# A two-layer network behind a linear-attention scan: all eight first-layer banks by float32r parts, VectorE makes the parts of x, attention buffers shared, new order from step 3 on

## The chip, the cores and the metric

The kernel runs on one core of one Trainium2 chip. The metric is device time in microseconds (us) of one execution. The kernel before takes 586.06 us, the median of 3 runs (585.86 to 586.9).

## The reference

An attention block with a decaying state is followed by a network of two layers. Shapes: 4 batches, 8 heads, 768 positions, 48 dimensions a head; 3072 tokens of 384 features; 2048 hidden units. All is float32.

```python
f = 1.0 / (1.0 + np.exp(-f_logit))
for t in range(S):
    state = f[:, :, t, :, None] * state + np.einsum('bhd,bhe->bhde', k[:, :, t], v[:, :, t])
    y[:, :, t] = np.einsum('bhd,bhde->bhe', q[:, :, t], state)
...
x = y.transpose(0, 2, 1, 3).reshape(B * S, H * D)
h = x @ w_in
g = np.maximum(h, 0.0) + alpha * np.minimum(h, 0.0)
return g @ w_out
```

## The kernel before

**Steps.** The work is cut into 12 steps, numbered 0 to 11. A step is a pair of batches and a chunk of 128 positions: 256 tokens. Each step has an attention part and a network part. The attention of step n+1 runs among the network of step n.

**Order.** Every engine runs its instructions in the order of one list, `ORDER_WORDS`, written out in the program. A word such as `5R0` is the part `R0` of step 5; `5Nb3` is the part `b3` of step 5's network; words without a number (`Y3`, `Z3`, `S3`, `W2`, `T`) prepare the weights. A part that yields is spread over several words of the same name. Each word issues on one engine or queue, so the list fixes the order on TensorE, VectorE, ScalarE, GpSimd and SyncE alone, and waits between engines follow from who reads and writes which bytes. Transfers are issued from SyncE's queue (outputs, turned keys, x) and from GpSimd's queue (loads of f, q, k, v for the steps after the first).

**Attention.** Words that the change and the prediction touch:

- `ef`, `eq`, `ek`, `ev`: loads of f, q, k, v (L369, L386). `f` (L396 to L403): sigmoid of f on ScalarE and three copies. `F` (L410 to L421): products of neighbouring decays on VectorE. `g` (L439 to L444): ScalarE copies to the first part of `scores`. `G` (L458, L462): scans over blocks of four, which read a constant pattern `ones`.
- `h`, `i`, `k` (L469, L490, L500, L496, L504, L578): scaled keys and queries and, from step 2 on, VectorE's transpose of the keys; it goes into the buffer in which f was. `K` (L584): the turned keys go through DRAM.
- `p`, `q` (L544): from step 2 on, six products that write queries shifted by one to seven quarters into `scores`. `u0`, `u1` (L705): 64 instructions on TensorE that multiply keys with these. `r0`, `r1` (L696): the same for positions within a quarter.
- `R0`, `R1` (L715) and `U0`, `U1` (L560): VectorE's predicated copies of both results from PSUM into the small buffer `ad`. `A0`, `A1` (L724): ScalarE copies `ad` into the score matrix `A`.
- `d` (L648), `D`, `M` (L659, L666): increments of the state and its update. `y` (L733), `Y` (L602): the outputs y. `X` (L611 to L614): y goes through DRAM to the layout `xT`, 384 features by 256 tokens (the last step by ten smaller transfers, L747).

**Network.** The hidden layer is cut into eight banks of 256 units. A bank is six products of 128 by 128 weights with 256 columns of x (L955) in one PSUM bank. In steps 0 to 2 all banks are plain float32 (`Na`). From step 3 on (`PARTS = 3`) banks 2 to 7 (`SPLIT = 2, 8`) are computed from float32r parts in three passes: `hi` with the high part of x, `lo` with the low part (both `Na`), a scaling of the bank in place on ScalarE (`Nq`, L969), and `sum` with a mix of x (`Nb`). Banks 0 and 1 stay plain. The parts of the weights are made once (`Y`, `Z`, `S`: L896, L900, L902, L906).

The parts of x are made in each step: `Nx` (ScalarE, L941) rounds x to `xh`; `Ny` and `Nz` (ScalarE, L944) copy it scaled to `xl` and `xs`; `NY` and `NZ` (L947) are accumulating transfers from GpSimd's queue that add x to `xl`, and `xl` to `xs`.

Behind each bank ScalarE writes the negative side (`Nr`, L979) and VectorE the gate in two halves (`Nc`, L986). The second layer is done with seven block products of 16 instructions each (`Np`, L1013) of sums of gate blocks (`Nm`, `Nu`, `Nv`, `Nw`, L1007). VectorE and ScalarE gather the results in `o` (L1023, L1044, L1048); `NL` is the last of these. `Ns0` and `Ns1` store `o` (L891) from SyncE's queue.

Of the kernel before, what the change touches and what calls it, by code (L numbers as in the profile page):

```python
# [8 lines left out]
F32 = mybir.dt.float32  # L9
F32R = mybir.dt.float32r  # L10
# [8 lines left out]
C = 128  # L19
# [3 lines left out]
U = 2  # L23
# [12 lines left out]
SPLIT = 2, 8  # L36
TURNED = SPLIT[1] - SPLIT[0]
# [4 lines left out]
0ef 0eq 0ek 0ev 0ev a0 a1 0f a2 0f 0F b0 0f a3 0F 0F 0F 0F 0I0 0F 0g 0g 0G 0G 0r1 0g 0G 0G 0g 0r0 1ef 0g 0I1 0g 0h 0I2  # L42
a0 0I3 0I4 a0 0i 0I5 a1 0m a4 1eq a1 0p 0p 1ek 0p 0p a2 1ev b1 0p 0j 1ev a2 0l 0o a5 0l 0O 0R0 0O 0k 0O 0R0 0O 0R0 0R0
0q 0q 0u0 0s 0s 0s 0t 0s w0 0t 0J0 0K0 0U0 0U0 0J1 0U0 0R1 0H0 0H0 0R1 0J2 0H0 0R1 0H0 1f 0R1 w1 0u1 1f 1f 0K1 0J3 0U1
2ef 0A0 0U1 0A0 0U1 1F 0d 0A0 1F 0A0 1F 0J4 0D 1F 0D 0J5 1F 0H1 0H1 1F 0H1 0H1 w2 0A1 0y0 0A1 1G 1G 0A1 0J6 0A1 1G 1G
0Y0 b0 0y1 b0 0x0 0M 2ev 0Y1 a6 2ev 1g 0M 1g 0J7 0M 1g 1r0 1g 1i 1g 0x1 1g 1R0 1R0 0X 0X 1R0 1r1 0X 1R0 a3 1h 0Na0 a3
a4 2eq a7 w3 a4 2ek 1m 0Na1 b1 b2 w4 b1 1R1 1R1 a5 a6 0Na3 1p 1p 1p b3 a6 1R1 1p 1j 1R1 1s 0Nr1 0Nr3 a5 1s 0Nc1 0Nc3
0Nc3 0Na2 w5 1p 1t 2f 0Nc1 b4 0Na4 w6 0Nr2 0Nc2 1l a7 0Nr4 0Nc2 0Na5 1t 1s 1l 1k 1s a7 b2 w7 0Nr0 1K1 1o 0Nc4 0Nr5
0Nc5 b2 b4 0Nc0 0Na6 1O 1O 1O 0Na7 b3 0Nc0 v0 1q 0Nc5 b4 v1 b7 0Np0 0Nr6 1K0 0Nc4 b5 b5 1q 1u0 b3 v2 1O v3 1U0 1u1 1U0
1U0 b5 1U1 2f 2f 2F 1H0 1H0 2F 1H0 1H0 2g 2F 2F 2F 0Np1 2g 2f b7 1U1 0Nc6 b6 b7 2F 2G v4 v5 1d v7 0Nr7 b6 2g 0Np2 2G  # L50
2g 1D 1D b6 1U1 1A0 2h 2p 1H1 2p 1H1 V 1H1 0Nc7 0Nc7 1H1 0Nc6 v6 W1 W0 2q 1A0 1A0 W3 1A0 0Np3 0Np4 0Np5 2q 1y0 W2 1A1
1A1 1A1 1A1 2h Y2 2g 2q 1y1 1Y1 1Y0 0Np6 1M 0Np7 2q 2u0 1M 2G 2G 1M W4 2i 1X 1X 1X 1X 1X 1X 1X 1X 1X 2r0 2R0 1X 2i
1Na1 2R0 2i 2R0 2R0 2U0 2U0 2U0 2k Y4 2k 1Nr1 0No1 0No0 2U0 2U0 1Na2 2U0 1Nr2 Y3 2U0 2A0 1Na0 3ef 2l 2l W6 2r1 1Nr0 2l
W5 2A0 1Nc1 2K 1Nc0 2A0 1Nc0 2o 2t 2K 2l 1Na5 2D 2K 2l 1Nr5 1Nc5 1Na4 1Nc1 Z4 Z4 1Na3 2t 1Nc5 2O 2A0 2R1 Z2 2R1 1Na6
# [105 lines left out]
def kernel(  # L160
# [985 lines left out]
```

## Time and profile before

| what | value |
|---|---|
| median of 3 runs | 586.06 us |
| the profiled execution's own time | 585.39 us |
| its span, from first to last instruction | 583.6 us |
| mean granted TensorE clock | 0.985 |
| GpSimd, accumulating transfer to `xl` (L947) | 9 of 934 ns on the queue |
| ScalarE, idle before rounding x (L941), ended by the transfer of x | 23.9 us in 8 waits |

PE is TensorE's matmuls, PEld its weight loads, DVE VectorE, ACT ScalarE, POOL GpSimd, SP SyncE. The digits of a slice are tenths of busy time in a fortieth of the span. In a group's row stand line, engine, operation, output and inputs by their names, shapes and count, then busy us and the mean ns of one, then the idle time before them and what ended it. Matmuls overlap, so one that lasts 380 ns does not hold TensorE for 380 ns: what counts is the time from one start to the next.

### The profile page before, as it was taken

What the parts mean: (1) busy time and instruction counts of PE and PEld (TensorE: products, weight loads), DVE (VectorE), ACT (ScalarE), POOL (GpSimd) and SP (SyncE); (2) the same over time, 40 slices, a digit from 0 to 9 for tenths busy, and PEclk for the clock granted to TensorE, in tenths of its full rate; (3) what the DMA queues carried; (4) which work ended last, traced back from release to release, by engine and by line L of the source; (5) the groups of instructions that cost most, each with busy time, mean ns of one, the idle gap of its engine ahead of it and who ended that gap; (6) DMA issues with size and microseconds to landing.
All of it is one profiled execution on the core that took longest, in us unless ns stands there. A gap on an engine that the chain in (4) does not pass through costs nothing.

```text
span 583.6 us, 19142 instructions
## 1 busy us (share of the span) xinstructions
PE 570.9 (98%) x8308; PEld 525.9 (90%) x8308; DVE 499.5 (86%) x1055; ACT 317.6 (54%) x593; POOL 63.4 (11%) x104
## 2 busy tenths in 40 slices
PE   8799999999999999999999999999999999999997
PEld 6678767899899899999899999999999999999997
DVE  6888799999999899999999899989998979864262
ACT  5698883673372582483384284385384284372230
POOL 5202000200100111111010100111111100101000
PEclk9679999999999999999999999999999999999999
DMA  9938501630713553543633542743542641512200
GB/s 287 357 120 297 218 1 57 164 90 12 190 35 82 93 173 96 113 154 104 134 110 80 105 150 66 151 145 88 105 155 62 136 150 55 93 52 65 60 1 27
DMA packets 69444, 67.59 MB, mean 116 GB/s; under 512 B 44688, under 2 KB 58640, under 8 KB 69360
## 3 DMA queue, kind: packets, MB, share of 16 engines
q1 hardware_dynamic: 59744, 37.16, 22.9%
q0 software_dynamic: 8880, 28.84, 18.7%
q8 instruction: 65, 1.06, 0.7%
q10 hardware_dynamic: 736, 0.37, 0.2%
q14 instruction: 19, 0.16, 0.1%
HBM read 44.99 MB, written 13.50 MB: 100 GB/s over the span
## 4 chain that ended last, share of the span: by engine, by line
PE 65%; DVE 14%; ACT 2%; DMA 2%; issue 2%; SPq 0%; DVEq 0%; POOLq 0%
PE ph L955 28%; PE pa L1013 8%; PE pc L1013 4%; PE pb L1013 4%; PE pf L1013 4%; PE pe L1013 4%; PE pd L1013 4%; PE py L733 3%; PE qu L705 3%; DVE scores L544 2%; DVE gate L1007 2%; PE raw L696 2%; PE inc L648 2%; DMA f<-in_fT 1%; DMA turned<-f 1%
## 5 line engine op out<-in xcount | busy, mean ns | idle before, releaser
L979 ACT ACTIVATE gate<-ph 128x512 f32<-128x512 f32 x96 | 56.0, 596 | 107.0 <-PE ph L955 77.4
L986 DVE SCALAR_TENSOR_TENSOR gate<-gate,om,ph 128x256 f32<-128x256 f32 x192 | 84.9, 474 | 26.8 <-ACT gate L979 26.2
L1007 DVE TENSOR_TENSOR gate<-gate 128x512 f32<-128x512 f32 x88 | 59.1, 685 | 13.2 <-PE pb L1013 6.3
L955 PE MATMUL ph<-xT,w_in_sb 128*128 128x256 f32 x288 | 66.0, 380 | 0.0
L1013 PE MATMUL pa<-w_out_sb,gate 128*128 128x192 f32 x352 | 61.3, 327 | 0.0
L955 PEld LDWEIGHTS ph<-xT,w_in_sb 128*128 128x128 f32 x288 | 53.7, 190 | 6.9 <-issue 0.2
L1013 PEld LDWEIGHTS pa<-w_out_sb,gate 128*128 128x128 f32 x352 | 57.4, 190 | 0.3
L969 ACT ACTIVATE ph<-ph 128x512 f32<-128x512 f32 x54 | 30.7, 579 | 38.0 <-PE ph L955 32.0
L955 PE MATMUL ph<-xh,hi 128*128 128x256 f32 x324 | 49.0, 288 | 1.9 <-DVE o L1023 1.0
L955 PE MATMUL ph<-xT,w_in_split 128*128 128x256 f32 x216 | 48.6, 381 | 0.0
L560 DVE COPY_PREDICATED ad<-inq,qu 128x224 f32<-128x224 int32 (+6 forms) x140 | 41.9, 300 | 7.0 <-PE qu L705 3.6
L955 PE MATMUL ph<-xl,lo 128*128 128x256 f32 x324 | 47.7, 285 | 0.0
L955 PEld LDWEIGHTS ph<-xh,hi 128*128 128x128 f32 x324 | 42.4, 190 | 4.2 <-issue 1.5
L955 PEld LDWEIGHTS ph<-xT,w_in_split 128*128 128x128 f32 x216 | 40.6, 190 | 5.6
L955 PE MATMUL ph<-xs,sum 128*128 128x256 f32 x324 | 44.0, 281 | 0.0
L955 PEld LDWEIGHTS ph<-xl,lo 128*128 128x128 f32 x324 | 42.6, 191 | 0.3
L724 ACT COPY A<-ad 32x256 f32<-32x256 f32 x88 | 35.3, 401 | 10.7 <-DVE ad L560 9.5
L715 DVE COPY_PREDICATED ad<-mraw,raw 128x256 f32<-128x256 int32 (+1 forms) x88 | 38.9, 442 | 2.6 <-ACT A L724 0.7
L955 PEld LDWEIGHTS ph<-xs,sum 128*128 128x128 f32 x324 | 40.1, 188 | 0.6 <-ACT ph L969 0.2
L544 DVE TENSOR_TENSOR scores<-scores,q 128x768 f32<-128x768 f32 (+5 forms) x60 | 37.3, 621 | 0.8
L1013 PE MATMUL pb<-t,gate 128*128 128x192 f32 x176 | 31.0, 330 | 0.0
L1013 PE MATMUL pc<-t,gate 128*128 128x192 f32 x176 | 30.8, 328 | 0.0
(150 smaller groups left out, 1067.4 us busy)
## 6 DMA issues: line engine op xcount, KB each, us to landing
w_out_raw<-in_w_out SPq DMA_DIRECT2D x8, 767.8 KB, 11.8
w_in_raw<-in_w_in SPq DMA_DIRECT2D x8, 767.2 KB, 10.6
f<-in_fT POOLq DMA_DIRECT2D x11, 512.0 KB, 6.9
q<-in_qT POOLq DMA_DIRECT2D x11, 512.0 KB, 5.9
k<-in_kT POOLq DMA_DIRECT2D x11, 512.0 KB, 6.3
turned<-f SPq DMA_DIRECT2D x40, 128.0 KB, 3.4
ksn<-turned SPq DMA_DIRECT2D x10, 512.0 KB, 4.0
out<-o SPq DMA_DIRECT2D x24, 192.0 KB, 3.7
```

What stands on the lines that cost most here:

```text
L544: nc.vector.tensor_tensor(by_four(us[:, :, UO[m]:UO[m] + 4 * n]), by_four(us[:, :, skip:skip + 4 * n]), spread(fq[:, :, 1:1 + n], n), ALU. ...
L560: nc.vector.copy_predicated(to, inq[:, 0:NB - m].bitcast(I32).unsqueeze(1).unsqueeze(3) .broadcast_to((128, H, NB - m, 4)), of)
L705: nc.tensor.matmul(qu[DB * j:DB * (j + 1), par, hp * QS + 4:hp * QS + QL], lhsT=x["k4"][r_, g * DB:(g + 1) * DB], rhs=x["us"][r_, g, 4:QL] ...
L715: nc.vector.copy_predicated(adu[:, :, :, d:4], diag[:, :, 0:n].bitcast(I32).unsqueeze(1).broadcast_to((128, H, NB, n)), rv[:, :, QO[d]:QO[ ...
L724: nc.scalar.copy(A[s_, u, :, s_], ad[s_].rearrange("p r h t -> p (r h) t"))
L733: nc.tensor.matmul(py[64 * par:64 * par + 64, u, o:o + CH], lhsT=vs_flat[bp][:, at_:at_ + 64], rhs=A[:, u, par * HP + hp, CH * cc:CH * (cc ...
L955: nc.tensor.matmul(banks[f][:, j * T:(j + 1) * T], lhsT=of[:, kt, 128 * j:128 * (j + 1)], rhs=by[:, kt], start=first_ and kt + j == 0, sto ...
L969: nc.scalar.activation(banks[f], banks[f], AF.Copy, scale=EPS - 1.0)
L979: nc.scalar.activation(to, of, AF.Relu, scale=-1.0)
L986: nc.vector.scalar_tensor_tensor(to[:, j], to[:, j], om[:, m:m + 1], of[:, j], ALU.mult, ALU.add)
L1007: nc.vector.tensor_tensor(block(to)[:, p], block(x_)[:, p], block(y_)[:, p], op)
L1013: nc.tensor.matmul(banks[to][:, 0:DH], lhsT=block(of)[:, f], rhs=of_w_out(by)[:, f], start=start and f == 0, stop=f == NH - 1, skip_group_ ...
```

## The change

All eight banks are computed by parts from step 3 on, so banks 0 and 1 get `hi`, `lo` and `sum` as well, two scalings a step more, and six more products of weight preparation. `xl` goes: VectorE makes the low part in the place of x (`NY`) and the mix (`NZ`); the two copies `Ny`, `Nz` and the accumulating transfers go.

To make room, buffers are shared. `scores` becomes four segments of 1024 columns: seven shifted queries lie in 28 of each 32 columns; `ad` lies in the four columns left over in segments 1 and 2; f is loaded into segment 3. The transposed keys go into q's buffer, `kh` into `q3`'s first part, and the scans' `ones` into spare columns of q's buffer, written by ScalarE in each step. The output `o` of a step uses the buffer of the mix `xs`. Part `i` gives one of its operations to `k`. The signs of the high parts are turned, so that the remaining operations are additions. The order list is new from the middle of step 1's attention on; ahead of that only the loads `1ef` and `2ef` stand later.

```diff
-SPLIT = 2, 8
-TURNED = SPLIT[1] - SPLIT[0]
+PIECES = 8
...
+    SEG = DB - 4
+    PLACES = {1: (0, 4), 2: (1, 4), 7: (1, 28), 3: (2, 4), 6: (2, 24), 4: (3, 4), 5: (3, 20)}
...
+    scores = const.tile([128, 4 * W], F32, tag="scores", name="scores")
+    segs = scores.rearrange("p (s g t) -> p s g t", s=4, t=DB)
...
+    ad = scores.rearrange("p (h i t) -> p h i t", i=NB, t=DB)[:, 4:12, :, 0:4]
...
-            t = work.tile([128, W], F32, tag=name, name=f"{name}_{i}", bufs=1)
+            t = scores[:, 3 * W:4 * W] if name == "f" else work.tile([128, W], F32, tag=name, name=f"{name}_{i}", bufs=1)
...
-            nc.scalar.copy(x["fs"][:, 0:NS:NB + 1], ones[:, 1:2].broadcast_to((128, G + 1)))
+            nc.scalar.copy(x["fs"][:, 0:NS:NB + 1], one[:, 1:2].broadcast_to((128, G + 1)))
+            yield
+            nc.scalar.copy(x["ones"].rearrange("p (g i) -> p g i", i=NB + 1), one.unsqueeze(1).broadcast_to((128, G // 2, NB + 1)))
...
+                        nc.tensor.matmul(qu[DB * j:DB * (j + 1), par, hp * C:hp * C + 4 * SEG].rearrange("p (s t) -> p s t", s=4),
+                                         lhsT=x["k4"][r_, g * DB:(g + 1) * DB], rhs=segs[r_, :, g, 4:DB], start=True, stop=True)
...
         def fourth():
+            ended(1, x)
+            yield
+            started(1, x)
+
+        def fifth():
             ended(0, x)
             yield
-            ended(1, x)
-            yield
-            started(1, x)
-
-        def fifth():
             carried(x)
             yield
-            nc.vector.transpose(x["kt"], x["ks"].rearrange("p g s t -> p (g s t)"))
+            nc.vector.transpose(x["q"], x["ks"].rearrange("p g s t -> p (g s t)"))
...
         def high_of_x():
-            nc.scalar.activation(late["xh"], x["T"], AF.Copy, scale=ROUND)
-
-        def part_of_x(to, scale):
-            nc.scalar.activation(late[to], late["xh"].bitcast(F32), AF.Copy, scale=scale)
-
-        def rest_of_x(to, of):
-            nc.gpsimd.dma_start(out=late[to].bitcast(F32), in_=of.bitcast(F32), accum_op=ALU.add)
...
+            nc.scalar.activation(late["xh"], x["T"].bitcast(F32), AF.Copy, scale=-ROUND)
+
+        def low_of_x():
+            nc.vector.tensor_tensor(x["T"], x["T"].bitcast(F32), late["xh"].bitcast(F32), ALU.add)
+
+        def mix_of_x():
+            x["xs"] = late["parts"].tile([128, NK, T], F32R, tag="xs", name=f"xs_{i}")
+            nc.vector.scalar_tensor_tensor(x["xs"], late["xh"].bitcast(F32), -EPS, x["T"].bitcast(F32), ALU.mult, ALU.add)
...
-            if by_parts(f):
-                products(f, late["hi"][:, f - SPLIT[0]], late["xh"], True, False)
+            if n_ >= PARTS:
+                products(f, late["hi"][:, f], late["xh"], True, False)
                 yield
-                products(f, late["lo"][:, f - SPLIT[0]], late["xl"], False, False)
+                products(f, late["lo"][:, f], x["T"], False, False)
...
+        def side_(r):
+            if "o" not in x:
+                x["o"] = late["parts"].tile([128, U, DM], F32, tag="xs", name=f"o_{i}")
+            return x["o"][:, r]
...
-            parts.update(x=high_of_x, y=lambda: part_of_x("xl", -1.0), z=lambda: part_of_x("xs", EPS),
-                         Y=lambda: rest_of_x("xl", x["T"]), Z=lambda: rest_of_x("xs", late["xl"]))
+            parts.update(x=high_of_x, Y=low_of_x, Z=mix_of_x)
```

The list itself is over a thousand words long. Three places of it are spoken of below. The stretch from step 9's last output word to step 10's mix, new:

```
9NL 9Ns0 11l 11r1 11l 11t 11t 11t 11l 11t 10Na1 11U0 11l 11U0 10NY 10Na3 10Na4 10Na4 10NZ
```

The words of step 10's network behind the last `11U1`, old, then new (words of step 11 left out):

```
Nc0 Nr4 Nc0 Nr3 Nb2 Na5 Nc4 Nr2 Na6 Nc3 Na6 Nq6 Nc4 Na7 Nq5 Na7 Nc2 Nc3 Nb6 Nb5 Nq7 Nr5 Nc2 Nb7 Nc5 Nc5 Nr7 Nr6 Nc6 Nc6 Nc7 Nc7 Np0 Nm0 Np2 Nu0 Nv0 Nk Np3 Ng Nm1 Nu1 Nv1 Np1 Nw0 Nw1 Np6 Np4 Np5 Nd Ne Nf Nh Nj Nl Ni NL Ns0 Ns1
Nr5 Nc6 Nc6 Nb7 Nr7 Nc7 Np0 Nc7 Nm1 Nc5 Nc5 Np2 Nu0 Nv0 Nk Nu1 Np3 Np1 Nw0 Nw1 Np6 Nv1 Np4 Nd Ne Ng Nh Nj Np5 Nf Ni Ns1 Nl NL Ns0
```

The load of f of step 10 stands as `9u0 ... 9u1 ... 10ef 10f`, with the other words of step 9 and of step 8's network between them.

More of the change, by code (lines that the diff above doesn't have):

```diff
@@ L50 @@
[L50 to L54, printed above, removed]
@@ L971, in third_pass @@
         def third_pass(f):
-            products(f, late["sum"][:, f - SPLIT[0]], late["xs"], False, True)
+            products(f, late["sum"][:, f], x["xs"], False, True)
         def sides(f):
```

289 lines of the change are left out of this document (144 added, 145 removed).

## The prediction

> **What bounds the kernel now.** I read the page first, then windows of busy time, then the order of time on TensorE.
>
> ```profile
> span 583.6 us, 19142 instructions
> ...
> PE 570.9 (98%) x8308; PEld 525.9 (90%) x8308; DVE 499.5 (86%) x1055; ACT 317.6 (54%) x593; POOL 63.4 (11%) x104
> ...
> PE   8799999999999999999999999999999999999997
> ...
> DVE  6888799999999899999999899989998979864262
> ...
> PE 65%; DVE 14%; ACT 2%; DMA 2%; issue 2%; SPq 0%; DVEq 0%; POOLq 0%
> ```
>
> TensorE is busy almost everywhere and carries 65% of the chain of waits. But VectorE's slices are also nines from 80 us to 510 us; its free time lies at both ends. The same in three stretches (columns: length, then busy us and instruction count of PE, PEld, DVE, ACT, POOL, then clock, DMA share, GB/s):
>
> ```profile
> 80.00:160.00 80.00, 79.74 (x1085) 67.98 (x1084) 77.99 (x158) 41.17 (x79) 7.22 (x11) 1.00 0.35 92
> 80.00:513.40 433.40, 430.12 (x6631) 401.08 (x6630) 403.78 (x866) 231.22 (x440) 46.33 (x63) 1.00 0.42 106
> 513.40:583.60 70.20, 66.75 (x563) 65.45 (x561) 30.58 (x67) 22.14 (x43) 2.86 (x4) 1.00 0.15 40
> ```
>
> I cut at 513.40 because VectorE's last attention copy of step 11 (word 11U1) ends there:
>
> ```profile
> 511.89 1.46 DVE L560 COPY_PREDICATED ad<-inq,qu 128x160 f32<-128x160 int32 x5
> ```
>
> Behind it stands a tail whose length TensorE sets (66.75 of 70.20). Ahead of it VectorE is busy 403.78 of 433.40, 93%, and from 80 to 160 us even 77.99 of 80, 97.5%, with TensorE at 79.74. So this is a kernel bound by TensorE with a second engine close behind, and the change takes from the first and gives to the second.
>
> **TensorE's gain per bank.** A first-layer bank is six products. In plain float32 each is two instructions, by parts three (parts of x times hi, lo, sum). Starts in order of time, from the tail, where nothing waits:
>
> ```profile
> 543.89 2.75 PE L955 MATMUL ph<-xT,w_in_sb 128*128 128x256 f32 x12
> 546.29 1.07 PE L955 MATMUL ph<-xh,hi 128*128 128x256 f32 x6
> 547.19 0.88 PE L955 MATMUL ph<-xl,lo 128*128 128x256 f32 x6
> 547.91 0.88 PE L955 MATMUL ph<-xh,hi 128*128 128x256 f32 x6
> 548.63 0.88 PE L955 MATMUL ph<-xl,lo 128*128 128x256 f32 x6
> 549.35 0.84 PE L955 MATMUL ph<-xs,sum 128*128 128x256 f32 x6
> 550.03 0.88 PE L955 MATMUL ph<-xh,hi 128*128 128x256 f32 x6
> ```
>
> A hi or lo pass takes 0.72 us from start to start (547.91, 548.63, 549.35), a sum pass 0.68 (549.35 to 550.03): 2.12 us per bank. The plain bank and the hi pass behind it take 3.30 (543.89 to 547.19), so the plain bank takes 3.30 - 0.72 = 2.58. Gain: 0.46 us per bank. Banks 0 and 1 change in steps 3 to 11, 18 banks: 8.3 us. The lower bound comes from the groups' own busy time, which charges the change of kind between groups to the parts:
>
> ```profile
> L955 PE MATMUL ph<-xT,w_in_sb 128*128 128x256 f32 x288 | 66.0, 380 | 0.0
> L955 PE MATMUL ph<-xh,hi 128*128 128x256 f32 x324 | 49.0, 288 | 1.9 <-DVE o L1023 1.0 <-DVE gate L986 0.6
> L955 PE MATMUL ph<-xl,lo 128*128 128x256 f32 x324 | 47.7, 285 | 0.0
> L955 PE MATMUL ph<-xs,sum 128*128 128x256 f32 x324 | 44.0, 281 | 0.0
> L955 PEld LDWEIGHTS ph<-xT,w_in_sb 128*128 128x128 f32 x288 | 53.7, 190 | 6.9 <-issue 0.2
> L955 PEld LDWEIGHTS ph<-xh,hi 128*128 128x128 f32 x324 | 42.4, 190 | 4.2 <-issue 1.5 <-ACT gate L979 1.4 <-ACT ph L969 0.4
> ```
>
> 66.0 / 24 banks = 2.75 against (49.0 + 47.7 + 44.0) / 54 = 2.61: 0.14 x 18 = 2.6 us. I take 8.3, since starts are what the next matmul sees. The quarter products keep 112 columns in four pieces of 28: no new price.
>
> The weight loads speak against the gain: 12 x 53.7 / 288 = 2.24 us of load time for a plain bank, 18 x 42.4 / 324 = 2.36 by parts. The Trainium skill, Perfetto Trace Analysis, Identifying the Most-Contended Engine, says that matmul busy time misjudges TensorE's headroom and that the busy share of weight loads is the better measure. By that rule the 18 banks would cost 18 x 0.12 = 2.2 us more instead of 8.3 less; the passes above, at 0.72 us for six loads whose own records are 190 ns each, speak against it.
>
> **VectorE's new work.** Today x's parts are made by two copies on ScalarE and two accumulating DMAs from GpSimd's queue. Now VectorE makes both: one two-input operation over 768 columns each.
>
> ```profile
> L902 DVE SCALAR_TENSOR_TENSOR lo<-w_in_split,lo 128x768 fp32r<-128x768 f32 x6 | 5.7, 950 | 0.0
> L906 DVE TENSOR_TENSOR sum<-lo,hi 128x768 fp32r<-128x768 f32 x6 | 5.8, 966 | 0.4 <-PE ph L955 0.4
> L986 DVE SCALAR_TENSOR_TENSOR gate<-gate,om,ph 128x256 f32<-128x256 f32 x192 | 84.9, 474 | 26.8 <-ACT gate L979 26.2
> L1007 DVE TENSOR_TENSOR gate<-gate 128x512 f32<-128x512 f32 x88 | 59.1, 685 | 13.2 <-PE pb L1013 6.3 <-PE pc L1013 6.0
> L659 DVE TENSOR_TENSOR vs<-vs,f 48x768 f32<-48x768 f32 x20 | 19.1, 953 | 1.8 <-PE py L733 1.3
> ```
>
> The two forms cost 0.95 us, as L902 and L906 show for the same size. Ahead of 11U1 lie steps 3 to 10: 16 x 0.95 = 15.2 us. The two further pieces of w_in need a lo and a sum each: 2 x (0.95 + 0.97) = 3.8. The transposed keys, the carried keys and the predicated copies keep their counts and sizes; only addresses change.
>
> **What the new order moves across the cut.** Behind the last 11U1 the old order has nine first-layer passes of step 10 (second pass of bank 5, both of 6 and 7, third of 2, 5, 6, 7); the new one has only the third of bank 7. That is 5 x 0.72 + 3 x 0.68 = 5.6 us of TensorE moved ahead of the cut. Seven gating operations go with them (7 x 84.9 / 192 = 3.1 us of VectorE), one half of a gate sum (0.67) and one state product (0.95). Step 11's increments (64 small matmuls) go behind it:
>
> ```profile
> L648 PE MATMUL inc<-vs,ksn 64*48 64x48 f32 x768 | 11.9, 213 | 0.2 <-ACT A L687 0.2
> ```
>
> That is 11.9 / 12 = 1.0 us back into the tail.
>
> **Work that costs nothing, and its cover.**
>
> ```profile
> L944 ACT ACTIVATE xl<-xh 128x768 fp32r<-128x768 f32 x9 | 7.5, 838 | 0.2
> L969 ACT ACTIVATE ph<-ph 128x512 f32<-128x512 f32 x54 | 30.7, 579 | 38.0 <-PE ph L955 32.0 <-DVE gate L986 2.8 <-ACT A L526 1.6
> L398 ACT COPY k<-f 128x256 f32<-128x256 f32 x12 | 8.0, 663 | 2.0 <-PE qu L705 1.7
> ```
>
> Per step ScalarE loses two copies like L944's (1.68 us) and gains two bank scalings (1.16) and one copy of ones, at most L398's 0.66. That is even; ScalarE is busy 231 of 433 us, and without that cover 0.2 us a step would show. The 18 accumulating DMAs leave GpSimd's queue, so its loads of f, q, k, v no longer stand behind them. That is a relief for a queue that sets nothing now. The new waits are these:
>
> ```profile
> f<-in_fT POOLq DMA_DIRECT2D x11, 512.0 KB, 6.9
> out<-o SPq DMA_DIRECT2D x24, 192.0 KB, 3.7
> xT<-tokens SPq DMA_DIRECT2D x9, 384.0 KB, 3.2
> ```
>
> f now lies in the fourth quarter of the scores buffer, so its load can start only when the previous step's quarter matmuls (u1) are through; in the order u1 stands some 6 us of VectorE work ahead of the load, and ScalarE's sigmoid 0 to 3 us behind it, except 13 us in step 4. With 6.9 us to landing, the sigmoid may wait 4 to 7 us. Queued behind it on ScalarE are gate and A copies; ScalarE has 200 us free in the stretch, so I take zero and keep 1 us a step, 8 us, as the other end. xT is now overwritten in place, so its next load waits for the last lo pass; at least 11 us of VectorE work between y's copy and the first part, in steps 3 to 10, cover the two transfers. The outputs share the mix's buffer: see the third rival.
>
> **The sum.** Ahead of the cut VectorE has 403.8 + 15.2 + 3.8 + 3.1 + 0.67 + 0.95 = 427.5 us. At the 97.5% of 80 to 160 us this takes 438.5, which is 5.1 more than 433.4; with no gap at all 427.5, 5.9 less. TensorE there has 430.1 - 16 x 0.46 + 5.6 - 1.0 = 427.3, which at 79.74 of 80 takes 428.7: 4.7 less, so this is the floor. I take 436, +2.5: nearer to the row that shows VectorE full, a little under it since the row holds waits as well. The tail loses 5.6 and step 11's 2 x 0.46 = 0.9, and gets 1.0 back: -5.5. Together -3.0 on the profiled execution's 585.39 us (span 583.6 and 1.8 around it): 582.4. The runs' median, 586.06, is 0.67 above that execution, so 583.0 us.
>
> **Rivals.** *First, VectorE's work finds its gaps.* With VectorE taking 428.7 or less, TensorE sets the stretch: -4.7 - 5.5 gives 575.2, with the offset 575.9. For it: TensorE missed only 0.26 us from 80 to 160 us although VectorE was full. Against: it needs VectorE above 99% for 430 us.
>
> *Second, the weight loads set the pace.* TensorE gains nothing and pays 2.2 us: 586.06 + 2.2 = 588.3, slower by 0.4%. The rule of the skill quoted above would have it so; the 0.72 us passes speak against it.
>
> *Third, slower: the mix waits for the store.* The mix of step n+1 is written where step n's output lies, so VectorE must wait until the last store has landed, 3.7 us after its issue. In the new order, between the word that finishes the output (NL) and the mix (NZ), little lies on VectorE. In step 10 it is this, with the first part's 0.95:
>
> ```profile
> L509 DVE TENSOR_TENSOR q<-q,q 128x512 f32<-128x512 f32 x10 | 6.9, 686 | 0.1
> L496 DVE TENSOR_TENSOR q<-scores,q 128x512 f32<-128x512 f32 x20 | 13.5, 675 | 0.0
> L560 DVE COPY_PREDICATED ad<-inq,qu 128x224 f32<-128x224 int32 x20 | 8.2, 409 | 4.0 <-PE qu L705 3.6
> ```
>
> With two copies near L560's 0.4 and two operations under 0.2 us that is 3.4 us; in steps 7 to 9 the same count gives about 3.6, in steps 4 to 6 between 4.3 and 5.0. Once VectorE is full, whatever is missing stops the attention copies and gate operations queued behind the mix, and so PSUM banks and TensorE. At 0.5 us for wake-up and issue besides the landing it is under 1 us a step; with SyncE's queue late, since each store stands behind a transfer that waits for another, 1 us in each of 8 steps: 583.0 + 8 = 591. It decides as soon as VectorE has no gap left to repay, and today's waits show that it is not free of them:
>
> ```profile
> DVE gate L986 <- ACT gate L979: 9.3, 14, 1.9
> DVE ad L560 <- PE qu L705: 3.6, 3, 1.9
> ```
>
> These are waits from 80 to 513.4 us (total, times, longest): 12.9 us in which VectorE already waits for ScalarE and TensorE.
>
> **How the numbers follow.** My forecast, VectorE as the second bound at 583.0 (its own range 580 to 587), has 0.45; the first rival 0.18, the second 0.07, the third 0.30. The time is the likeliest's. A change under 0.2%, 1.2 us, is not told from none here. Of the forecast's 0.45 some 0.30 is faster by more than that, 0.10 within and 0.05 slower; the first rival is all faster; the second is 0.02 within and 0.05 slower; the third 0.03 within and 0.27 slower. Faster 0.48, same 0.15, slower 0.37. The range reaches from just under the first rival to above the third: 575.5 to 593.5.
>
> **What would show it.** In the changed profile, 2.1 us from start to start for every bank of steps 3 to 11; VectorE near 520 us busy in all and at 97% from 160 us to the last 11U1; that word at about 516 us, then 65 us of tail. If VectorE waits for out's store ahead of the mix in most steps, the third rival holds. I am wrong altogether if ScalarE's sigmoid waits for f by more than it has free, or if VectorE stays under 95% while TensorE too falls below 97%.

## The result, and the profile after

The changed kernel takes 588.86 us, the median of 20 runs (587.04 to 591.13); the kernel before took 586.69 us beside it, 20 runs (585.26 to 589.14). The ratio is 1.0035, interval 1.0021 to 1.0049: slower by 0.35%. The forecast was 583.0 us, faster by 0.5%. The profiled execution took 590.55 us, with a span of 588.8 us. It lies 1.7 us above the median of its kernel, and the profiled execution of before (585.39 us) 1.3 us below the one beside it: some 3 of the 5.2 us by which the spans differ are spread between executions, and the stretches below hold them.

First the page of the changed kernel: busy time of each engine, slices of TensorE and VectorE, and the shares of the chain of waits.

```profile
span 588.8 us, 19396 instructions
...
PE 565.6 (96%) x8416; PEld 520.8 (88%) x8416; DVE 515.3 (88%) x1077; ACT 320.7 (54%) x607; POOL 50.2 (9%) x89
...
PE   8789989999999999989999999999999999999996
...
DVE  6888798989999999989999989999999999984452
...
PE 24%; DVE 11%; issue 1%; DMA 1%; ACT 0%; DVEq 0%; ACTq 0%; SPq 0%
```

TensorE lost 5.3 us of busy time (570.9 before), VectorE gained 15.8 (499.5), and the span grew by 5.2. TensorE's share of the chain fell from 65% to 24% (the shares of the new chain sum to 37%, so it was followed back only part of the way; TensorE to VectorE is 65 to 14 before and 24 to 11 after). Between 404 and 424 us the chain of the changed kernel, in order of time, is almost VectorE alone:

```profile
404.42 1.15 DVE scores L468
405.58 0.96 DVE scores L544
...
418.01 0.87 DVE xT L950
...
423.58 0.95 DVE xs L954
```

The last 11U1 and the windows on its two sides, in the columns of the prediction:

```profile
527.10 0.18 DVE L563 COPY_PREDICATED scores<-inq,qu 128x32 f32<-128x32 int32 x1
```

```profile
80.00:527.30 447.30, 438.41 (x6809) 408.04 (x6808) 423.62 (x898) 241.98 (x467) 31.46 (x47) 1.00 0.34 91
527.30:588.80 61.50, 56.96 (x502) 56.19 (x500) 26.77 (x57) 15.25 (x30) 1.03 (x2) 0.98 0.06 21
```

Against the rows of before:

| stretch | before | forecast | after |
|---|---|---|---|
| 80 us to the last 11U1 | 433.40 | 436 | 447.30 |
| VectorE busy in it | 403.78 | 427.5 | 423.62 |
| VectorE idle in it | 29.6 | 8.5 | 23.7 |
| TensorE busy in it | 430.12 | 427.3 | 438.41 |
| tail | 70.20 | 64.7 | 61.50 |

That is where the time went. VectorE got 19.8 us of work ahead of the cut; the stretch became 13.9 us longer, and only 5.9 us went into idle time that VectorE had. The tail gave 8.7 back. TensorE's idle time in the stretch grew from 3.3 to 8.9 us. Most of what is left of VectorE's idle time are waits (rows of the changed kernel, 80 to 527.3 us; total, times, longest):

```profile
DVE gate L990 <- ACT gate L983: 4.6, 7, 1.1
DVE qd L410 <- ACT qd L398: 3.0, 2, 1.5
DVE vs L670 <- PE inc L652: 2.6, 2, 1.7
```

The ten rows sum to 14.5 us. The same view of before has twelve rows that sum to 20.3 us, the first two of them in the prediction; the next two are

```profile
DVE gate L1007 <- PE pb L1013: 2.1, 3, 1.2
DVE qd L410 <- ACT qd L400: 1.8, 2, 1.5
```

So of the 29.6 us idle before, 9.3 were in no wait that the view lists; after, it is 23.7 - 14.5 = 9.2. In the traces these are short gaps between one VectorE instruction and the next, 294 before and 280 after, each of at most 0.15 us and most of 0.02 to 0.05. That part did not shrink; the waits shrank from 20.3 to 14.5.

TensorE has 11 us more in the stretch than was forecast. Part of it came from the head, where it does less than before (before, then after), and part from the tail, as shown further below. In the head it is ten products of an early step's second layer (L993 before, L997 after: 31 of them ahead of 80 us, then 21) that moved into the stretch:

```profile
0.00:80.00 80.00, 74.05 (x1119) 59.40 (x1120) 65.13 (x125) 64.27 (x112) 14.19 (x37) 0.89 0.68 233
```

```profile
0.00:80.00 80.00, 70.26 (x1109) 56.53 (x1110) 64.90 (x124) 63.51 (x112) 17.68 (x40) 0.92 0.68 233
```

### The profile page after: what moved, and what is told of

It reads as the page before. It is cut to its first block, busy times and chain, and to the rows that moved or that the text cites. A ratio compares the mean times of both kernels' runs of the same rounds, so it can differ in the third digit from the quotient of the medians.

```text
span 588.8 us, 19396 instructions
## 1 busy us (share of the span) xinstructions
PE 565.6 (96%) x8416; PEld 520.8 (88%) x8416; DVE 515.3 (88%) x1077; ACT 320.7 (54%) x607; POOL 50.2 (9%) x89
## 3 DMA queue, kind: packets, MB, share of 16 engines
q0 software_dynamic: 6288, 21.76, 12.3%
## 5 line engine op out<-in xcount | busy, mean ns | idle before, releaser
L990 DVE SCALAR_TENSOR_TENSOR gate<-gate,om,ph 128x256 f32<-128x256 f32 x192 | 82.4, 474 | 14.5 <-ACT gate L983 14.0
L959 PE MATMUL ph<-xh,hi 128*128 128x256 f32 x432 | 61.9, 286 | 1.4 <-DVE gate L990 0.9
L959 PE MATMUL ph<-xT,lo 128*128 128x256 f32 x432 | 59.3, 280 | 0.1
L959 PEld LDWEIGHTS ph<-xh,hi 128*128 128x128 f32 x432 | 54.6, 189 | 4.1 <-issue 1.7
L959 PE MATMUL ph<-xs,sum 128*128 128x256 f32 x432 | 56.1, 280 | 1.3 <-DVE xs L954 1.0
L959 PEld LDWEIGHTS ph<-xT,lo 128*128 128x128 f32 x432 | 54.2, 188 | 0.7 <-DVE xT L950 0.3
L526 ACT COPY A<-q 48x512 f32<-48x512 f32 x44 | 27.2, 618 | 47.9 <-DVE q L496 47.5
L563 DVE COPY_PREDICATED scores<-inq,qu 128x224 f32<-128x224 int32 (+6 forms) x140 | 42.2, 301 | 3.6 <-PE qu L553 0.7
L718 DVE COPY_PREDICATED scores<-mraw,raw 128x256 f32<-128x256 int32 (+1 forms) x80 | 35.6, 445 | 1.9 <-PE raw L700 0.9
L730 ACT COPY A<-scores 32x256 f32<-32x256 f32 x80 | 32.1, 401 | 3.5 <-DVE scores L563 2.5
L410 DVE TENSOR_TENSOR qd<-qd,scores 128x768 f32<-128x768 f32 (+2 forms) x36 | 27.2, 755 | 4.9 <-ACT qd L398 4.8
```

What stands on the lines that cost most here:

```text
L410: nc.vector.tensor_tensor(qdv[d], qdv[d - 1][:, :, :, 1:5 - d], f[:, :, 1:5 - d].rearrange("p (g i) r -> p g i r", i=NB), ALU.mult)
L526: nc.scalar.copy(A[halves(cc)[1], :, par * HP:(par + 1) * HP, CH * cc:CH * (cc + 1)], x["q3"][rows(par)].rearrange("p (u h c) s t -> p u h ...
L563: nc.vector.copy_predicated(ad[:, :, m:NB], inq[:, 0:n].bitcast(I32).unsqueeze(1).unsqueeze(3) .broadcast_to((128, H, n, 4)), of.rearrange ...
L718: nc.vector.copy_predicated(ad[:, :, :, d:4], diag[:, :, 0:n].bitcast(I32).unsqueeze(1).broadcast_to((128, H, NB, n)), rv[:, :, QO[d]:QO[d ...
L730: nc.scalar.copy(A[s_, u, :, s_].rearrange("p h (i t) -> p h i t", t=4), ad[s_])
L959: nc.tensor.matmul(banks[f][:, j * T:(j + 1) * T], lhsT=of[:, kt, 128 * j:128 * (j + 1)], rhs=by[:, kt], start=first_ and kt + j == 0, sto ...
```

## The experiments

Ratios are to the kernel before, run on the same chip; a difference of two ratios is given in us of 586.7, with the two intervals added as squares. Edits are to the changed kernel unless another is named.

**VectorE's work, less and more**

*e1: Both parts off VectorE.*

```diff
-            nc.vector.tensor_tensor(x["T"], x["T"].bitcast(F32), late["xh"].bitcast(F32), ALU.add)
+            nc.vector.tensor_tensor(x["T"][:, 0, 0:128], x["T"][:, 0, 0:128].bitcast(F32), late["xh"][:, 0, 0:128].bitcast(F32), ALU.add)
...
-            nc.vector.scalar_tensor_tensor(x["xs"], late["xh"].bitcast(F32), -EPS, x["T"].bitcast(F32), ALU.mult, ALU.add)
+            nc.scalar.activation(x["xs"], late["xh"].bitcast(F32), AF.Copy, scale=-EPS)
```

> The changed kernel, with the low part made over 128 of 768 columns only and the mix made by one scaled copy on ScalarE (the rest of the low part, and the low part within the mix, are left out). This takes some 1.75 us a step from VectorE, 14 us ahead of the last attention copy of step 11, and adds 0.84 us a step to ScalarE. Theory V (VectorE sets the pace of the changed kernel): the time falls by 6 to 12 us, to 577 to 583. Theory P (TensorE still sets the pace, and the loss comes from waits that the new order builds in): within 1.5 us of the changed kernel's 588.9. Theory S (the mix waiting for the output's store): within 2 us too, since the mix still waits, on ScalarE.

Ratio 0.9936 (0.9906 to 0.9965): 5.8 us (± 1.9) faster than the changed kernel, and faster than before. The windows of 160 to 520 us, the changed kernel first, then this one:

```profile
160.00:520.00 360.00, 352.19 (x5565) 335.32 (x5564) 341.77 (x732) 190.36 (x370) 24.15 (x36) 1.00 0.35 95
```

```profile
160.00:520.00 360.00, 355.15 (x5725) 339.60 (x5724) 334.34 (x732) 200.26 (x389) 23.67 (x35) 1.00 0.35 93
```

TensorE gets 160 more instructions through in the same 360 us. VectorE has 14.7 us less to do on x's parts: 17.3 (rows L954 and L950 further below) less 2.6 for the narrow low part,

```profile
L950 DVE TENSOR_TENSOR xT<-xT,xh 128x128 fp32r<-128x128 f32 x9 | 2.6, 294 | 0.0
```

so the added VectorE work costs time, 0.4 us for one us. The edit also takes the mix's wait for the store off VectorE; e5 below finds that this wait is worth little.

*e2: The mix twice.*

```diff
+            for _ in range(2):
-            nc.vector.scalar_tensor_tensor(x["xs"], late["xh"].bitcast(F32), -EPS, x["T"].bitcast(F32), ALU.mult, ALU.add)
+                nc.vector.scalar_tensor_tensor(x["xs"], late["xh"].bitcast(F32), -EPS, x["T"].bitcast(F32), ALU.mult, ALU.add)
```

> The changed kernel with the mix of x made twice on VectorE, 0.95 us more a step in steps 3 to 11. Theory V: 0.9 x 8 = 7 us slower than the changed kernel, 595 to 597. Theory P: under 2 us slower. Theory S: under 2 us slower.

Ratio 1.0137 (1.0104 to 1.0171): 6.0 us (± 2.2) more for 9 x 0.96 = 8.6 us of VectorE work. The price of one such us is 0.7.

**TensorE's work, less and more**

*e3: Third passes of banks 0 and 1 left out.*

```diff
-                products(f, late["lo"][:, f], x["T"], False, False)
+                products(f, late["lo"][:, f], x["T"], False, f < 2)
...
+            if f >= 2:
-            products(f, late["sum"][:, f], x["xs"], False, True)
+                products(f, late["sum"][:, f], x["xs"], False, True)
```

> The changed kernel without the third passes of banks 0 and 1 (these twelve products a step are left out of the result): 12 x 9 x 0.114 = 12.3 us less on TensorE, nothing else changed. Theory P: 8 to 12 us faster than the changed kernel, 577 to 581. Theory V: 1.4 us of it (step 11, in the tail) and little more, 586 to 588.

Ratio 1.0081 (1.0052 to 1.0111), 2.7 us (± 1.9) more than the changed kernel; the spans of the profiled executions are 588.9 us and 588.8. TensorE has 108 products less and nothing is gained. Why it even comes out slower stays open. The windows of 160 to 520 us, and of 80 us to the last 11U1:

```profile
160.00:520.00 360.00, 341.79 (x5463) 323.82 (x5462) 340.98 (x732) 189.65 (x370) 23.70 (x36) 1.00 0.36 94
```

```profile
80.00:527.50 447.50, 428.43 (x6713) 397.06 (x6712) 423.13 (x898) 241.06 (x467) 31.49 (x47) 1.00 0.34 91
```

VectorE is as busy as in the changed kernel (340.98 of 341.77), with the same 732 instructions; TensorE simply idles 10 us more. The stretch is as long as in the changed kernel (447.5 against 447.3) with 10 us less of TensorE's work in it. So this work of TensorE does not set the pace, nor do its weight loads, of which 108 are gone too.

*e4: Banks 0 and 1 plain again.*

```diff
-            if n_ >= PARTS:
+            if n_ >= PARTS and f < 2:
+                products(f, late["hi"][:, f].bitcast(F32), late["xh"].bitcast(F32), True, True)
+            elif n_ >= PARTS:
...
-            nc.scalar.activation(banks[f], banks[f], AF.Copy, scale=EPS - 1.0)
+            if f >= 2:
+                nc.scalar.activation(banks[f], banks[f], AF.Copy, scale=EPS - 1.0)
```

(the third pass as in the edit above)

> The changed kernel with banks 0 and 1 plain float32 again (from the high parts alone, so the low parts of these two banks are left out of the result), their scaling and third pass gone: TensorE 0.46 x 18 = 8.3 us more, ScalarE 1.2 us a step less, VectorE as in the changed kernel. Theory P: 6 to 8 us slower than the changed kernel, 595 to 597. Theory V: the tail's 0.9 us and at most 2 more, 589 to 592. If the part passes gain nothing at all on TensorE: 588 to 590.

Ratio 1.024 (1.0211 to 1.0269), 12.0 us (± 1.9) more than the changed kernel, more than any theory had. The gain of 18 banks by parts, 18 x 0.48 = 8.6 us (2.58 us for a plain bank as in the prediction, 2.10 by parts as shown in the next section), would explain some 70%. The rest may come from long passes at places of an order built round short ones; that is argued, not shown. The run also says that more work on TensorE costs, although e3 found nothing in less. Both can be true if the changed kernel lies where the two limits meet, so that more work on either engine costs and less on one leaves the other; e2, e3 and e4 fit this, and no run tests it alone.

*e10: Both relieved*: the edits of the first and of the third experiment together.

> The changed kernel with the parts taken off VectorE as in the first run (ratio 0.9936) and the third passes of banks 0 and 1 left out as in the third run (1.0081): 14 us less VectorE and 12.3 us less TensorE. If the two bound each other in turn, as theory V has it for a kernel that is balanced: ratio 0.975 to 0.985, since TensorE's work counts once VectorE is out of the way. If a third thing (latency of the chain from bank to gate, transfers) sets the pace: 0.990 to 0.995, no gain over the first run.

Ratio 0.9939 (0.9916 to 0.9963), as the first experiment alone (0.9936). With VectorE's parts gone, 12.3 us less on TensorE still bring nothing. Its longest waits, TensorE's and then VectorE's, from 160 to 520 us:

```profile
PE inc L652 <- DMA ksn<-turned: 2.7, 2, 1.6
PE ph L959 <- ACT gate L984: 1.7, 2, 0.9
```

```profile
DVE gate L991 <- ACT gate L984: 5.6, 10, 1.2
DVE qd L410 <- ACT qd L398: 5.0, 5, 1.7
```

TensorE waits for ScalarE, VectorE waits for ScalarE, and TensorE for keys on their way through DRAM, which VectorE's transpose starts: many short waits, none above 2 us. That they form a loop from engine to engine is read from these rows; no run takes one link out alone.

**The rival of the store**

*e5: Stores of steps 3 to 10 left out.*

```diff
-            s1=lambda: store(U * bp + 1, c, side_(1)),
-            s0=lambda: store(U * bp, c, side_(0)),
+            s1=lambda: None if 3 <= n_ <= 10 else store(U * bp + 1, c, side_(1)),
+            s0=lambda: None if 3 <= n_ <= 10 else store(U * bp, c, side_(0)),
```

> The changed kernel without the stores of the outputs of steps 3 to 10 (these outputs are left out), so that the mix of x waits for nothing but VectorE's and ScalarE's own work on the shared buffer. Theory S (the mix waits for the store, 1 us a step and all that is queued behind it): 5 to 8 us faster than the changed kernel, ratio to the kernel before 0.990 to 0.995. Theory V (VectorE's own work and its other waits): under 2 us faster, ratio 1.000 to 1.004; the profile of the changed kernel shows 3.0 us of this wait in all.

Ratio 1.0011 (0.999 to 1.0033): 1.4 us (± 1.5) less. In the changed kernel the wait of the mix for the store was

```profile
DVE xs L954 <- DMA out<-o: 3.0, 2, 2.1
```

two times in the whole trace, 3.0 us. The third rival's 8 us are not there.

**Another engine for the parts**

*e6: Low part on GpSimd* (`nc.gpsimd.tensor_tensor` in place of `nc.vector.tensor_tensor`).

> The changed kernel with the low part of x made on GpSimd instead of VectorE, complete and with the same result. VectorE loses 0.96 us a step, GpSimd gains one two-input operation over 768 columns, whose time no run has shown yet. Theory V: 0.8 of the 7.7 us ahead of the last copy comes back if GpSimd is done within 2 us, ratio 0.995 to 1.000; if GpSimd takes over 4 us, the mix queued behind on VectorE waits for it and the ratio is 1.005 or more. Theory P: 1.002 to 1.005.

Ratio 1.0094 (1.0061 to 1.0128), slower than with VectorE by 3.5 us (± 2.1), although GpSimd took 2.2 us for an operation, near the 2 us at which a gain was expected. VectorE lost 8.6 us of work, and its busy time rose, from 515.3 to 518.1 us; the last section shows why.

*e7: Mix by a ScalarE copy and a GpSimd addition.*

```diff
-            nc.vector.scalar_tensor_tensor(x["xs"], late["xh"].bitcast(F32), -EPS, x["T"].bitcast(F32), ALU.mult, ALU.add)
+            nc.scalar.activation(x["xs"], late["xh"].bitcast(F32), AF.Copy, scale=-EPS)
+            nc.gpsimd.tensor_tensor(x["xs"], x["xs"].bitcast(F32), x["T"].bitcast(F32), ALU.add)
```

> The changed kernel with the mix made by a scaled copy on ScalarE and an addition on GpSimd, complete. VectorE loses 0.96 us a step; the third passes, which stand 0 to 2 us of VectorE work behind the mix in the order, get it later by ScalarE's 0.84 us and GpSimd's time. Theory V: VectorE gains 6 us, TensorE waits for the mix: ratio 0.995 to 1.003. Theory P: TensorE's new wait of 2 to 4 us a step counts in full, ratio 1.02 or more.

Ratio 1.0304 (1.0267 to 1.034). TensorE's wait for it:

```profile
PE ph L960 <- POOL xs L955: 13.9, 9, 2.2
```

It takes 1.5 us more in each of nine steps, just ahead of a third pass. The kernel is 15.8 us (± 2.3) slower than the changed one, so this wait of TensorE counts in full, as theory P had it. VectorE, with 8.6 us of work less, then waits for ScalarE's negative sides of the banks, from 160 to 520 us 16.6 us instead of 3.5:

```profile
DVE gate L991 <- ACT gate L984: 16.6, 15, 2.9
```

A delay on TensorE thus comes back to VectorE.

*e8: Both edits together.*

> The changed kernel with the low part on GpSimd and the mix on ScalarE and GpSimd, complete: VectorE loses all of the 1.9 us a step, as in the run that left most of the parts out (ratio 0.9936). Theory V: 0.994 to 1.000, the difference being what the parts' later arrival costs TensorE. Theory P: 1.01 or more.

Ratio 1.0353 (1.0306 to 1.04): 18.7 us (± 2.9) more than the changed kernel, about the sum of the two (3.5 and 15.8). What GpSimd's operations do to VectorE stands in the last section.

**VectorE's work in the old order**

*e9: Kernel before, with fourteen small additions a step.*

```diff
             nc.scalar.activation(late[to], late["xh"].bitcast(F32), AF.Copy, scale=scale)
+            for _ in range(7):
+                nc.vector.tensor_tensor(late["spare"], late["xh"][:, 0, 0:72].bitcast(F32), late["xh"][:, 1, 0:72].bitcast(F32), ALU.add)
```

> The kernel before, old order and all, with fourteen small additions a step on VectorE into a spare buffer (7 at each of the words Ny and Nz, 72 columns each, some 2 us a step together; ScalarE's and GpSimd's parts stay). Theory V (VectorE was already so near its limit that new work on it counts): 8 x 2 us less what its waits absorb, ratio 1.010 to 1.025. Theory P: under 1.004, the work falls into VectorE's gaps, of which the stretch from 80 to 513 us has 30 us.

Ratio 1.0535 (1.0511 to 1.056): 31.4 us for 29.1 us of work.

```profile
L947 DVE TENSOR_TENSOR spare<-xh 128x72 f32<-128x72 f32 x126 | 29.1, 231 | 6.0 <-ACT xh L942 2.2
```

It was more work than the change brings (3.2 us a step, not 2), at another place: directly behind the rounding of x. So it gave a price for that place and left the change's own open. The next two tell it, with a kernel that has room for them.

*e12: The kernel before, with direct passes.* A bank by parts is now hi·xh + lo·xh + hi·xl: no mix, no sum of weights, no scaling; the product of both low parts is left out.

```diff
-                products(f, late["lo"][:, f - SPLIT[0]], late["xl"], False, False)
+                products(f, late["lo"][:, f - SPLIT[0]], late["xh"], False, False)
...
-            nc.scalar.activation(banks[f], banks[f], AF.Copy, scale=EPS - 1.0)
+            pass
...
-            products(f, late["sum"][:, f - SPLIT[0]], late["xs"], False, True)
+            products(f, late["hi"][:, f - SPLIT[0]], late["xl"], False, True)
```

> The kernel before with the same direct passes for its six banks: no scaling, no second accumulating transfer, no sums; VectorE loses 5.8 us once and nothing a step, TensorE's passes are as many. If the kernel before is bound by TensorE alone: within 2 us, ratio 0.996 to 1.001. If the chain from second pass over the scaling to the third holds TensorE up: 0.985 to 0.995.

Ratio 0.9969 (0.9955 to 0.9982).

*e13: That kernel, with the low part by VectorE*, in the place of the accumulating transfer:

```diff
-            parts.update(x=high_of_x, y=lambda: part_of_x("xl", -1.0), z=lambda: None,
-                         Y=lambda: rest_of_x("xl", x["T"]), Z=lambda: None)
+            parts.update(x=high_of_x, y=lambda: None, z=lambda: None,
+                         Y=low_of_x, Z=lambda: None)
```

> The kernel of e12_direct_passes_old (585.65 us) with one edit: the low part of x is made by one VectorE subtraction in the place where its accumulating transfer was issued; the scaled copy on ScalarE and the transfer go. VectorE gets 9 x 0.96 = 8.6 us more. Theory V (in the old order VectorE has no gap that can take work, as e9 showed for small operations at another place): the whole counts, 8 to 9 us, about 594 us. Rival T (TensorE sets the pace and the work falls into VectorE's idle time): within 2 us of 585.65. Half of it, 588 to 591, would say that e9's price was one of its place.

Ratio 1.0041 (1.0023 to 1.006): 4.2 us (± 1.3) for 8.6 us of work. Neither theory's number but half of V's, which had been named as the sign that the price of e9 belonged to its place.

*e14: And with the mix too*, into a buffer that no pass reads, so that TensorE cannot wait for it.

```diff
-                         Y=low_of_x, Z=lambda: None)
+                         Y=low_of_x, Z=mix_of_x)
```

> As e13_old_order_low_on_vector, and the mix too is made by VectorE, in the place where its transfer was issued, into a buffer of its own that no pass reads. VectorE gets 9 x 1.92 = 17.3 us more than in e12_direct_passes_old; this is the second part of the change by itself, in the old order and without shared buffers. Theory V: 8 to 9 us more than e13, about 602 us if that is at 594; then the new order, which carries the same work at 588.9 with eight banks by parts, is worth some 10 us, and the change is slower only because VectorE's work costs more than the order brings. Rival T: within 3 us of 585.65, and then the new order or the shared buffers cost the time.

Ratio 1.0155 (1.0124 to 1.0187): 6.7 us (± 2.2) more. The two operations cost 10.9 us (± 2.1) of 17.3 in the old order; the mix's part of it is the price of VectorE's time, since nothing waits for its result.

```profile
160.00:520.00 360.00, 350.55 (x5483) 331.29 (x5481) 331.69 (x709) 153.38 (x300) 24.25 (x36) 1.00 0.33 91
```

Here VectorE is 92% busy from 160 to 520 us, TensorE 97%; before it was TensorE that was full (99%).

**The version that beats both**

*e11: Direct passes in the changed kernel:* the same three passes for all eight banks; VectorE makes the low part only. The mix goes, and with it the eight sums of weight parts, ScalarE's scaling of the banks and the mix's wait for the store.

```diff
-            nc.vector.scalar_tensor_tensor(x["xs"], late["xh"].bitcast(F32), -EPS, x["T"].bitcast(F32), ALU.mult, ALU.add)
+            pass
...
-                products(f, late["lo"][:, f], x["T"], False, False)
+                products(f, late["lo"][:, f], late["xh"], False, False)
...
-            nc.scalar.activation(banks[f], banks[f], AF.Copy, scale=EPS - 1.0)
+            pass
...
-            products(f, late["sum"][:, f], x["xs"], False, True)
+            products(f, late["hi"][:, f], x["T"], False, True)
```

> The changed kernel with another three passes per bank: hi with xh, lo with xh, hi with the low part; the product of both low parts, some 2 to the minus 24 of the result, is left out. So the mix (0.96 us a step on VectorE), the eight sums of weight parts (0.97 each), the scaling of each bank in place (4.6 us a step on ScalarE, between the second and third pass) and the output's shared buffer's wait go; TensorE's passes are as many as before. Theory V: 15 us less VectorE, the ratio falls to 0.985 to 0.993. Theory P: 0.998 to 1.004.

581.87 us, ratio 0.9914 (0.9897 to 0.9931): 5 us faster than before, 7.1 us (± 1.3) faster than the changed kernel. How much of it is the mix's is not told apart; in the old order the scalings and the sums gave 1.8 us (e12).

```profile
160.00:520.00 360.00, 356.56 (x5757) 342.29 (x5758) 334.60 (x730) 162.46 (x319) 23.60 (x35) 1.00 0.35 94
```

*e15: Without the low part*, as in the first experiment (128 of 768 columns).

> The kernel of e11_direct_passes (581.87 us) with the low part of x made over 128 of its 768 columns only (the rest of xT stays as it is, so the third pass uses the wrong x there). VectorE has about 0.7 us a step less. Theory V (VectorE still sets the pace there): 4 to 6 us less, about 577. Rival T (with 99% busy TensorE sets the pace again): within 1.5 us of 581.9.

Ratio 0.9891 (0.9861 to 0.9921): 1.3 us (± 2.0) less.

*e16: Without the third passes of banks 0 and 1.*

> The kernel of e11_direct_passes (581.87 us) without the third passes of banks 0 and 1 (x's low part is left out there). TensorE has 18 x 0.68 = 12.3 us less. Rival T (TensorE sets the pace again): 6 to 12 us less, 570 to 576. Theory V (VectorE and the order set the pace as in e3): within 2 us of 581.9.

Ratio 0.9899 (0.9862 to 0.9935): 0.9 us (± 2.3) less. Theory V's 4 to 6 us for e15 did not come, nor rival T's 6 to 12 for e16. In the version with direct passes neither engine's work alone sets the pace: of some 6 us off VectorE (9 x (0.96 - 0.29)) and of 12.3 off TensorE hardly anything shows. TensorE's 99% busy share had promised otherwise.

## Why the prediction was wrong

**The step that failed** is the value taken for the stretch ahead of the last 11U1: "I take 436, +2.5". It was 447.3. The busy time behind it was not the fault: 427.5 forecast, 423.6 measured, with 0.96 us for each new operation as in the rows of the weights:

```profile
L954 DVE SCALAR_TENSOR_TENSOR xs<-xh,xT 128x768 fp32r<-128x768 f32 x9 | 8.7, 964 | 3.1 <-DMA out<-o 3.0
L950 DVE TENSOR_TENSOR xT<-xT,xh 128x768 fp32r<-128x768 f32 x9 | 8.6, 958 | 0.0
```

Of the 3.9 us between them 2.8 are the gating operations: six moved ahead of the cut, not seven, and the group's busy time stayed at 66.9 us (66.6 before), since more of them overlap. The fault was the idle time put on top, 8.5 us of a former 29.6; 23.7 us remained. I took the 8.5 from the row of 80 to 160 us, 97.5% busy: a share a little above that (427.5 of 436 is 98%), carried over 436 us. Over the whole stretch the changed kernel keeps VectorE at 94.7%, and the limit that the prediction itself named, "if VectorE stays under 95% while TensorE too falls below 97%", was half reached (TensorE is at 98.0%). Two facts of before spoke against 436 and were not used. The short gaps between VectorE's instructions, 9.3 us, alone exceed the 8.5 that were left. And the waits were for ScalarE and TensorE, whose work starts from VectorE's results; e7 shows such a wait growing when TensorE is delayed. The experiments show what such idle time takes: of 17.3 us added in the old order 6.4 vanished, of 19.8 in the change 5.9. TensorE's own 438.41 us in the stretch are above 436 too, but they are not what made it long: in e3 they are 428.43, and the stretch is 447.5.

**TensorE's gain per bank was right, and taking still more work off it brought nothing.** From the tail of the changed kernel, in a row of passes without a wait:

```profile
559.67 0.86 PE L959 MATMUL ph<-xT,lo 128*128 128x256 f32 x6
560.36 0.87 PE L959 MATMUL ph<-xh,hi 128*128 128x256 f32 x6
561.07 0.86 PE L959 MATMUL ph<-xs,sum 128*128 128x256 f32 x6
561.77 0.87 PE L959 MATMUL ph<-xh,hi 128*128 128x256 f32 x6
```

That is 0.69 + 0.71 + 0.70 = 2.10 us a bank, as forecast. Yet 12.3 us less on TensorE (e3) brought nothing. The 8.3 us themselves are needed: without the gain of banks 0 and 1 the kernel is 12.0 us slower (e4). What failed is to count such a gain as if the stretch could follow it.

**The tail** was forecast at -5.5 and came to -8.7. The term of moved passes was too small. I counted nine passes of step 10 behind the last 11U1 in the list; in the old trace TensorE was further behind VectorE than the list has it:

```profile
L955 PE MATMUL ph<-xs,sum 128*128 128x256 f32 x72 | 9.8, 280 | 0.0
L955 PE MATMUL ph<-xl,lo 128*128 128x256 f32 x60 | 8.8, 283 | 0.0
L955 PE MATMUL ph<-xh,hi 128*128 128x256 f32 x55 | 8.4, 286 | 0.0
L955 PE MATMUL ph<-xT,w_in_sb 128*128 128x256 f32 x24 | 5.5, 379 | 0.0
```

(tail of before, by groups.) 211 products, of which step 11 has 132: 79, or 13 passes. In the tail of after

```profile
L959 PE MATMUL ph<-xh,hi 128*128 128x256 f32 x48 | 7.1, 283 | 0.0
L959 PE MATMUL ph<-xs,sum 128*128 128x256 f32 x54 | 6.8, 276 | 0.0
L959 PE MATMUL ph<-xT,lo 128*128 128x256 f32 x48 | 6.7, 278 | 0.0
```

are 150, of which step 11 has 144: one pass, as in the list. Twelve passes left the tail, not eight: four times 0.7 is 2.8 us. Step 11's increments, which were to bring 1.0 us back, brought none, for all 64 of them ran in the tail already (before, then after):

```profile
L648 PE MATMUL inc<-vs,ksn 64*48 64x48 f32 x64 | 0.9, 207 | 0.0
```

```profile
L652 PE MATMUL inc<-vs,ksn 64*48 64x48 f32 x64 | 0.9, 207 | 0.0
```

Against these 3.8 us TensorE's idle time in the tail grew by 1.1 (70.20 - 66.75 before, 61.50 - 56.96 after), and the tail came out 3.2 shorter than forecast. The 2.8 went into the stretch ahead, as did the 3.8 that the head lost, and the 1.0 was taken off the stretch without being in it; of TensorE's 11 us there, 3.5 stay without a source in moved work. Longer busy records (last section) may be it; that is not shown. Before, TensorE ran four passes behind the list at the last 11U1; now it is level with it: it has caught up and waits.

**What cost nothing did.** ScalarE's sigmoid waited 0.8 us in the stretch for f in its new place:

```profile
ACT scores L394 <- DMA scores<-in_fT: 0.8, 2, 0.6
```

The zero taken for it was right, the 8 us kept as the other end were not needed.

**The rivals.** The first needed VectorE above 99%; it is at 94.7%. The third is refuted by e5 and by its row. The second, the weight loads, gave 588.3 us and so nearly the measured time, but by luck, for the runs deny its reason. The Trainium skill, Perfetto Trace Analysis, Identifying the Most-Contended Engine, takes the busy share of weight loads as a measure of TensorE's headroom, and the rival made a pace of it. Here their busy time fell from 525.9 to 520.8 us while the time rose, a bank takes 2.10 us instead of 2.58, and 108 loads less changed nothing (e3).

**The account.** From the kernel before: direct passes -1.8 us (e12), VectorE's two operations +10.9 (e13 and e14), and from there to the changed kernel 1.0155 to 1.0035, -7.0 us (± 2.1): the new order, two more banks by parts and the shared buffers, less what the mix and the scalings cost. Sum +2.1. So, by the price of the old order, the other parts of the change do gain, and VectorE's two operations take more than they give. How the 7.0 is divided among order, banks and buffers stays open: e4 took the banks back inside an order made for them, and the buffers were not tried alone.

The price of one us on VectorE is not one number: 0.4 from e1 to the changed kernel (5.8 of 14.7 us), 0.7 from there on (e2); in the old order 0.5 for the first operation and 0.8 for the second. In both orders the later work costs more, as if the price rose while VectorE fills; the intervals overlap, so this is not shown. A forecast of the stretch by 0.6 of the added 23.7 us would have been 433.4 + 14.2 = 447.6; that is said after the event.

## What to carry to other kernels

Where a second engine is over 90% busy behind the first, its idle time is not room: ask of each wait whether what it waits for would come earlier, and if both engines wait for each other through a third, charge added work at about half its time or more (0.4 to 0.8 here). A row from a short full stretch is a rate reached there, not one that can be held. Dropping work by other passes (the mix, with the sums and scalings) was worth more here than any choice of the engine that does it; GpSimd as the place for it was the worst.

## What the runs showed of the hardware

**A GpSimd operation stops VectorE's operations with two inputs in SBUF.** In the run with the low part on GpSimd, in order of time:

```profile
231.81 1.81 POOL L950 TENSOR_TENSOR xT<-xT,xh 128x768 fp32r<-128x768 f32 x1 [7.71 <-ACT xh L947]
231.95 2.22 DVE L500 TENSOR_TENSOR ks<-k,q 128x512 f32<-128x512 f32 x1
...
234.36 0.68 DVE L496 TENSOR_TENSOR q<-scores,q 128x512 f32<-128x512 f32 x1
```

L496, of the same size, takes 0.68 us; L500 takes 2.22: it starts 0.14 us behind GpSimd's and ends 0.55 behind its end. Where VectorE was in such an operation first, it was GpSimd's that grew, from 1.81 to 2.84 us:

```profile
324.61 0.69 DVE L509 TENSOR_TENSOR q<-q,q 128x512 f32<-128x512 f32 x1
324.75 2.84 POOL L950 TENSOR_TENSOR xT<-xT,xh 128x768 fp32r<-128x768 f32 x1 [23.60 <-ACT xh L947]
325.21 0.69 DVE L496 TENSOR_TENSOR q<-scores,q 128x512 f32<-128x512 f32 x1
```

So the operation was taken off VectorE's list and still stood in its way, for twice as long (2.2 us on average instead of 0.96):

```profile
L950 POOL TENSOR_TENSOR xT<-xT,xh 128x768 fp32r<-128x768 f32 x9 | 20.0, 2224 | 147.8 <-ACT xh L947 147.8
```

The Trainium skill, SBUF — State Buffer, SBUF: two separate sides, says that a VectorE operation with two SBUF inputs and a GpSimd operation lock each other out of a shared pair of ports, and whichever starts first keeps it. The first place agrees. In the second, L509 had it first, and L496, which starts behind it and 0.46 us after GpSimd's operation, is not held up either (0.69 us): VectorE's next operation came ahead of the one that waited. Not all of VectorE's work is held up: a transpose, which has one input, took its usual 1.25 us beside a GpSimd addition in e7 (L581 at 340.93 us).

**Busy time of TensorE is not a constant of its work.** The kernel before with small VectorE additions runs the same 8308 products, and its busy time is longer by 6.8 us (570.9 before) at nearly the same mean granted clock (0.983, and 0.985 before):

```profile
PE 577.7 (94%) x8308; PEld 528.3 (86%) x8308; DVE 527.8 (86%) x1181; ACT 317.6 (52%) x593; POOL 63.2 (10%) x104
```

Why the records grow is not shown. A busy share of 99% is thus no proof that TensorE sets the pace; taking its work away tells it (e3, e16).
